# Attention and gated MLP in float32: start addresses of matmul operands modulo 512 bytes, and an order of the first wave with sums and exponentials one step behind what feeds them

## The chip, the cores and the metric

One core of a Trainium2 chip runs the whole program. The metric is the device time of one execution in microseconds; the median of three runs is compared. The engines that matter here are TensorE (PE; its weight loads are PEld), VectorE (DVE), ScalarE (ACT), GpSimd (POOL, which here issues DMAs), and SyncE (SP, whose queue issues the other DMAs).

## The reference

Attention without a score matrix, and a gated MLP on its output, for 8 batches of 576 tokens (4608 tokens in all), 8 heads of 64, model width 512 and inner width 1536:

```python
q_s = exp(q - max(q, axis=-1));  q_s = q_s / (sum(q_s, axis=-1) + 1e-9)
k_s = exp(k - max(k, axis=2));   k_s = k_s / (sum(k_s, axis=2) + 1e-9)
kv  = einsum('bhsd,bhse->bhde', k_s, v)
x   = einsum('bhsd,bhde->bhse', q_s, kv)      # tokens x 512
gate = 1 / (1 + exp(-(x @ w_gate)))           # 512 -> 1536
out  = (gate * (x @ w_val)) @ w_out           # 1536 -> 512
```

## The kernel before

The 4608 tokens are nine **waves** of 512. A wave has its x (four blocks of 128 channels by 512 tokens, tile x_32), then the two up projections, the gate, and the down projection into four PSUM accumulators.

**Waves 1 to 8** keep precision by splitting each float32 operand into a high part and a remainder, both of type float32r, and by multiplying high by high, high by low and low by high (function prod, line 635, and line 703). A wave runs six steps, p = 0 to 5. Function g1 computes one step's two projections with seven products of half size instead of eight: the weights are three blocks as they are (tile a_w, kept in SBUF for all six steps) and four sums or differences of blocks (tile s_sb, one step at a time, read back from HBM by s_load right after its last use); the moving operands are c_hl, the x of the wave in seven parts. A product is 12 matmuls with 128 x 128 weights and 256 moving columns, a step 84 (line 635). Function g2 multiplies the result h of one step by the down weights: 24 matmuls (line 703), weights h, 512 moving columns of wo_hl, of which two tiles per step are read back from HBM: the first twelve matmuls stream one of tag wo_hl, the last twelve one of tag wo_t. Between the steps stand the matmuls that make the next wave's x: k_mm (line 358, weights k, moving v) and x_mm (line 518, weights kv_sb, moving the split q in tiles of the pool ring). Where a wave crosses a batch, x_mm works in two pieces of columns, and the second begins inside the tile: in wave 1 at column 64, byte 256.

**Wave 0** prepares all this. It runs plain float32 matmuls, 12 steps j: g1_0(j) (line 590), then g2_0(j - 1) (line 617), whose weights are h_0, the product of gate and value that VectorE makes in g_mul_0(j - 1) (line 602). Beside them each step narrows the next weights from 64-bit input words to float32 (w_low, w_top, w_join and their wo_ counterparts; narrow_sign on ScalarE, line 143), makes for each pair of steps the four sums (w_sums, line 235), splits sums and blocks into high and low (split_w, copies on ScalarE on line 222, subtractions on VectorE on line 223), saves s_sb to HBM (line 250), splits and saves wo (lines 201, 205), and computes the attention of wave 1 (after_first: the subtractions of q on line 433, the exponentials of q on 437, those of k on 293 and 337).

Nothing reorders instructions: each engine executes in the order in which the program is written (manual_schedule), and an instruction that waits holds all that stand behind it on its engine. Where a tile lies in SBUF follows from the order of the pools and of the tiles in them; the tiles named pad are never used, they only move what comes behind them.

## Time and profile before

| | |
|---|---|
| median of 3 runs | 1000.17 us (997.86 to 1000.83) |
| the profiled execution | 999.88 us, span 998.0 us |
| TensorE busy, its weight loads | 964.4 us, 832.2 us |
| VectorE, ScalarE, GpSimd busy | 610.5, 475.7, 167.4 us |
| matmuls of line 635, of line 703 | 4032 of 256 columns, 1152 of 512 |
| mean DMA rate | 258 GB/s |

The span runs from the first to the last instruction; the execution's own time is 1.9 us more. Times in rows are us from the start of the span unless ns is written. A duration of a matmul includes its way through the array, so that matmuls overlap in the record; how fast they follow each other is read from the starts.

### The profile page before, as it was taken

Reading aid. Unit: us, or ns where it says so; the run is one execution under the profiler, and the core shown is the slowest. Engines: PE = TensorE matmul, PEld = TensorE weight load, DVE = VectorE, ACT = ScalarE, POOL = GpSimd, SP = SyncE. Lnnn points to the kernel's source line nnn. Section 1 sums busy time; section 2 is a strip of 40 time slices with the busy share of each in tenths; the row PEclk is TensorE's granted clock in tenths of the full one; section 3 lists DMA queues with packets and bytes.
Section 4 is the critical chain, followed back from the end, with each engine's and each line's share of the span. In section 5 each row is a group of like instructions: output and inputs, shape, how many; then the busy total and the mean of one; then the engine's idle time right before and its main releaser. Section 6 shows DMA issues by size and latency. Waiting matters only on the chain.

```text
span 998.0 us, 15641 instructions
## 1 busy us (share of the span) xinstructions
PE 964.4 (97%) x6062; PEld 832.2 (83%) x6062; DVE 610.5 (61%) x1010; ACT 475.7 (48%) x815; POOL 167.4 (17%) x316
## 2 busy tenths in 40 slices
PE   5895999999999999999999999999999999999998
PEld 4432544699999999899999999999999999999997
DVE  8696778676566556745675567547663655463242
ACT  4679596453436254525453544353444434533222
POOL 0010001221122112112111111121212121212210
PEclk7998999999999999999999999999999999999999
DMA  9867567898699978997899789987998679858662
GB/s 347 311 173 309 227 240 214 294 353 271 198 236 360 306 223 194 375 294 242 166 384 321 236 151 379 321 255 139 385 304 231 212 227 314 241 178 252 191 207 73
DMA packets 93865, 257.79 MB, mean 258 GB/s; under 512 B 15264, under 2 KB 17568, under 8 KB 93024
## 3 DMA queue, kind: packets, MB, share of 16 engines
q0 software_dynamic: 43712, 168.32, 56.1%
q1 hardware_dynamic: 50080, 88.48, 29.7%
q8 instruction: 48, 0.79, 0.4%
q14 instruction: 25, 0.20, 0.1%
HBM read 228.20 MB, written 28.56 MB: 257 GB/s over the span
## 4 chain that ended last, share of the span: by engine, by line
PE 84%; ACT 8%; DMA 5%; DVE 2%; issue 1%; SPq 0%; ACTq 0%; DVEq 0%
PE gv L635 46%; PE acc L703 23%; PE gv L590 5%; PE acc L617 3%; PE at L358 3%; PE gv L518 2%; ACT ring L337 2%; DMA sg<-wv_in 1%; ACT ring L437 1%; DMA lent<-kT_in 1%; PE at L518 1%; ACT kt L293 1%; DMA ring<-k_in 1%; ACT L437 1%; DMA lent<-v_in 1%
## 5 line engine op out<-in xcount | busy, mean ns | idle before, releaser
L635 PE MATMUL gv<-c_hl,s_sb 128*128 128x256 f32 x2304 | 293.6, 283 | 1.8 <-ACT sg L653 1.8
L635 PEld LDWEIGHTS gv<-c_hl,s_sb 128*128 128x128 f32 x2304 | 283.6, 192 | 3.1 <-ACT sg L653 3.1
L703 PE MATMUL acc<-wo_hl,h 128*128 128x512 f32 x1152 | 274.5, 393 | 0.0
L703 PEld LDWEIGHTS acc<-wo_hl,h 128*128 128x128 f32 x1152 | 212.9, 188 | 47.2
L635 PE MATMUL gv<-c_hl,a_w 128*128 128x256 f32 x1728 | 231.4, 283 | 0.0
L635 PEld LDWEIGHTS gv<-c_hl,a_w 128*128 128x128 f32 x1728 | 220.2, 192 | 4.1 <-issue 0.7
L258 POOL DMA_DIRECT2D s_sb<-s x188 | 99.7, 530 | 330.1 <-PE gv L635 327.1
L661 DVE TENSOR_TENSOR sg<-gv,sg 128x512 f32<-128x512 f32 x48 | 33.2, 691 | 188.1 <-PE gv L635 188.1
L217 POOL DMA_DIRECT2D wo_hl<-wo x96 | 50.9, 530 | 304.4 <-PE acc L703 301.7
L663 ACT COPY sg<-gv 128x512 f32<-128x512 f32 x48 | 28.2, 587 | 110.1 <-PE gv L635 110.1
L590 PE MATMUL gv<-x,f_w 128*128 128x512 f32 x160 | 72.4, 605 | 4.7 <-ACT h L598 4.7
L653 ACT COPY sg<-gv 128x512 f32<-128x512 f32 x48 | 28.1, 585 | 101.9 <-PE gv L635 78.4
L665 DVE TENSOR_TENSOR sg<-sg 128x512 f32<-128x512 f32 x48 | 33.3, 693 | 61.9 <-ACT sg L663 61.9
L590 PEld LDWEIGHTS gv<-x,f_w 128*128 128x128 f32 x160 | 30.5, 194 | 43.1 <-issue 36.0
L686 DVE TENSOR_TENSOR h<-sg,h 128x1024 fp32r<-128x1024 f32 x48 | 58.8, 1226 | 1.6
L668 ACT ACTIVATE sg<-sg 128x512 f32<-128x512 f32 x48 | 30.4, 632 | 57.6 <-DVE sg L667 57.6
L617 PE MATMUL acc<-wo_t,h 128*128 128x512 f32 x96 | 46.4, 629 | 11.2 <-DVE h L602 11.2
L674 DVE TENSOR_TENSOR sg<-sg 128x512 f32<-128x512 f32 x48 | 33.2, 692 | 33.5 <-ACT sg L668 33.5
L617 PEld LDWEIGHTS acc<-wo_t,h 128*128 128x128 f32 x96 | 19.0, 202 | 36.3 <-issue 21.8
L658 ACT COPY sg<-gv 128x512 f32<-128x512 f32 x48 | 28.2, 587 | 43.6 <-PE gv L635 43.6
L655 ACT COPY sg<-gv 128x512 f32<-128x512 f32 x48 | 28.1, 586 | 32.3 <-PE gv L635 32.3
L667 DVE TENSOR_TENSOR sg<-gv,sg 128x512 f32<-128x512 f32 x48 | 33.2, 692 | 6.2
(151 smaller groups left out, 1021.1 us busy)
## 6 DMA issues: line engine op xcount, KB each, us to landing
s_sb<-s POOLq DMA_DIRECT2D x188, 512.0 KB, 6.7
wo_hl<-wo POOLq DMA_DIRECT2D x96, 512.0 KB, 5.7
s<-s_sb POOLq DMA_DIRECT2D x6, 2048.0 KB, 8.1
out<-x SPq DMA_DIRECT2D x36, 256.0 KB, 8.8
ring<-k_in SPq DMA_DIRECT2D x28, 256.0 KB, 14.3
ring<-qn_in SPq DMA_DIRECT2D x28, 256.0 KB, 9.8
q_b<-q_m_row SPq DMA_DIRECT2D x56, 128.0 KB, 7.9
ring<-qT_in SPq DMA_DIRECT2D x28, 256.0 KB, 9.2
```

The lines of the kernel that those rows point to most:

```text
L217: nc.gpsimd.dma_start(out=t.rearrange("p h e -> p (h e)"), in_=wo_dram[2 * p + i].bitcast(F32R))
L258: nc.gpsimd.dma_start(out=s_sb[:, i].rearrange("p h n e -> p (h n e)"), in_=s_dram[p][:, i * n:(i + 1) * n].bitcast(F32R),)
L590: nc.tensor.matmul(ps[n], lhsT=w[:, kt // 2, sl], rhs=x_0[:, kt], start=(kt == 0), stop=(kt == NK - 1),)
L617: nc.tensor.matmul(acc[0][m], lhsT=h_0[j][:, m * P:(m + 1) * P], rhs=wo_t[j // 2][:, j % 2], start=(j == 0), stop=(j == NJ - 1),)
L635: nc.tensor.matmul(ps[:, n], lhsT=lh(kt), rhs=c_hl[i][:, x, kt], start=(first and n == 0 and kt == 0 and lh is wh and x == 0), stop=(last ...
L661: nc.vector.tensor_tensor(out=sg[:, 0], in0=rr, in1=sg[:, 0], op=ALU.add)
L665: nc.vector.tensor_tensor(out=sg[:, 3], in0=sg[:, 3], in1=sg[:, 2], op=ALU.add)
L667: nc.vector.tensor_tensor(out=sg[:, 1], in0=z, in1=sg[:, 1], op=ALU.add)
L668: nc.scalar.activation(sg[:, 0:2, 0], sg[:, 0:2, 0], AF.Sigmoid)
L674: tt(out=sg[:, 0:2, 0], in0=sg[:, 0:2, 0], in1=sg[:, 0:2, 1], op=ALU.mult)
L686: nc.vector.tensor_tensor(out=lo, in0=sg[:, :, 0], in1=hi.bitcast(F32), op=ALU.subtract)
L703: nc.tensor.matmul(acc[w][m], lhsT=h[lh][:, i, sl], rhs=o[i][:, rh], start=(at == 0 and i == 0 and lh == 0 and rh == 0), stop=(at == NS - ...
```

## The change

It has two parts.

**Addresses.** The pools are put in another order, and two pads of 192 and 320 bytes a partition stand elsewhere, so that tiles begin at other addresses. Small tiles for the maxima of k get a pool of their own. No instruction changes by it. First byte of each tile within a partition, modulo 512, as the built programs have it:

| operand | used as | before | after |
|---|---|---|---|
| a_w, s_sb (line 635) | weights | 0 | 128 |
| c_hl (line 635) | moving | 0 | 448 |
| h (line 703) | weights | 0 | 128 |
| wo_hl, first of a step (line 703) | moving | 192 | 448 |
| wo_hl, second of a step, tag wo_t (line 703) | moving | 0 | 448 |
| kv_sb (line 518) | weights | 0 | 128 |
| q in ring (line 518) | moving | 0 | 448 |
| f_w, h_0 (wave 0) | weights | 0 | 128 |
| x_0, wo_t (wave 0) | moving | 0 | 448 |
| k in ring (line 358) | weights | 0 | 448 |
| v (line 358) | moving | 0 | 128 |

All slices that these matmuls take are multiples of 512 bytes into their tile, but for the second pieces of line 518.

**Order of wave 0.** split_w becomes split_hi (copies) and split_lo (subtractions). They run at steps 2, 4, 6, 8, 10 and 11 instead of 1, 3, 5, 7, 9 and 11, and split_hi stands ahead of the step's other work on ScalarE. The sums run at steps 1, 3, 5, 7, 9 and 10 instead of 0, 2, 4, 6, 8 and 10. The exponentials of q and the key sums of wave 1 move from step 2 to 3, the subtractions of k stay in 3, the sums over q move from 3 to 4. For odd j the sign bits of wo come from one more operation on VectorE (narrow_sign_bits) instead of one on ScalarE.

On ScalarE at steps 2 and 3, from the gate of step 2 (h_484 before, h_488 after; h_542 and h_538 are the gates of step 3) the order before is

```order
L598 ACTIVATE h_484<-gv 128x512
L437 ACT_TABLE_LOAD
L437 ACTIVATE ring<-ring 128x512 x4
L293 ACTIVATE lent,k_sum<-lent,k_neg 128x576 x4
L201 CAST wo_hl<-wo_t 128x512
L143 ACTIVATE w_raw<-w_raw 128x1024
L151 ACTIVATE f_w<-w_raw 128x2x256 x2
L143 ACTIVATE wo_raw<-wo_raw 128x512
L151 ACTIVATE wo_t<-wo_raw 128x512
L598 ACT_TABLE_LOAD
L598 ACTIVATE h_542<-gv 128x512
L222 CAST s_sb<-s_492 128x512
```

and after

```order
L615 ACTIVATE h_488<-gv 128x512
L215 CAST wo_hl<-wo_t 128x512
L147 ACTIVATE w_raw<-w_raw 128x1024
L162 ACTIVATE f_w<-w_raw 128x2x256 x2
L147 ACTIVATE wo_raw<-wo_raw 128x512
L162 ACTIVATE wo_t<-wo_raw 128x512
L615 ACTIVATE h_538<-gv 128x512
L454 ACT_TABLE_LOAD
L454 ACTIVATE ring<-ring 128x512 x4
L310 ACTIVATE lent,k_sum<-lent,k_neg 128x576 x4
L262 CAST s_sb<-s_547 128x512
L262 CAST s_sb<-s_548 128x512
```

The table load, the four exponentials of q (ring) and the four of k (lent) have moved behind the gate of step 3, and the copies of the split stand behind them.

On VectorE at step 10, from the product of step 10 (h_949 before, h_953 after) the order before is

```order
L602 TENSOR_TENSOR h_949<-gv,h_949 128x512
L205 TENSOR_TENSOR wo_hl<-wo_t,wo_hl 128x512
L235 TENSOR_TENSOR s_1001<-f_last 128x512
L235 TENSOR_TENSOR s_1002<-s_1001,f_last 128x512
L235 TENSOR_TENSOR s_1003<-f_last 128x512
L235 TENSOR_TENSOR s_1004<-f_last,s_1002 128x512
L560 TENSOR_TENSOR ring<-x_89 128x512
L560 TENSOR_TENSOR ring<-x_89,ring 128x512
L560 TENSOR_TENSOR ring<-x_89 128x512
L560 TENSOR_TENSOR ring<-x_89,ring 128x512
```

and after

```order
L619 TENSOR_TENSOR h_953<-gv,h_953 128x512
L219 TENSOR_TENSOR wo_hl<-wo_t,wo_hl 128x512
L266 TENSOR_TENSOR s_sb<-s_957,s_sb 128x512
L266 TENSOR_TENSOR s_sb<-s_958,s_sb 128x512
L266 TENSOR_TENSOR s_sb<-s_959,s_sb 128x512
L266 TENSOR_TENSOR s_sb<-s_960,s_sb 128x512
L266 TENSOR_TENSOR a_w<-f_w,a_w 128x2x512
L266 TENSOR_TENSOR a_w<-f_w,a_w 128x512
L243 TENSOR_TENSOR s_1012<-f_last 128x512
L243 TENSOR_TENSOR s_1013<-s_1012,f_last 128x512
L243 TENSOR_TENSOR s_1014<-f_last 128x512
L243 TENSOR_TENSOR s_1015<-f_last,s_1013 128x512
```

The subtractions of split 4 (s_sb, a_w) now stand between the save of wo_hl and the sums of the last pair; before, they stood ahead of the product.

The diff, without empty lines:

```diff
@@ -53,20 +53,25 @@
     nc = tc.nc
     const = ctx.enter_context(tc.tile_pool(name="const", bufs=1))
+    cpool = ctx.enter_context(tc.tile_pool(name="cpool", bufs=1))
+    apad = ctx.enter_context(tc.tile_pool(name="apad", bufs=1))
     apool = ctx.enter_context(tc.tile_pool(name="apool", bufs=1))
     two = ctx.enter_context(tc.tile_pool(name="two", bufs=2))
-    pad = ctx.enter_context(tc.tile_pool(name="pad", bufs=1))
-    pad.tile([P, 80], F32, name="pad_2")
+    wpad = ctx.enter_context(tc.tile_pool(name="wpad", bufs=1))
+    wpool = ctx.enter_context(tc.tile_pool(name="wpool", bufs=2))
     four = ctx.enter_context(tc.tile_pool(name="four", bufs=4))
     ring = ctx.enter_context(tc.tile_pool(name="ring", bufs=11))
+    small = ctx.enter_context(tc.tile_pool(name="small", bufs=2))
+    apad.tile([P, 48], F32, name="pad_a")
+    wpad.tile([P, 80], F32, name="pad_w")
     dpool = ctx.enter_context(tc.tile_pool(name="dpool", bufs=2, space=bass.MemoryType.DRAM))
     spool = ctx.enter_context(tc.tile_pool(name="spool", bufs=1, space=bass.MemoryType.DRAM))
     ps_acc = ctx.enter_context(tc.tile_pool(name="ps_acc", bufs=NT, space=bass.MemoryType.PSUM))
     ps_gv = ctx.enter_context(tc.tile_pool(name="ps_gv", bufs=3, space=bass.MemoryType.PSUM))
     ps_at = ctx.enter_context(tc.tile_pool(name="ps_at", bufs=1, space=bass.MemoryType.PSUM))
-    const.tile([P, 96], F32, name="pad_0")
     s_sb = const.tile([P, 4, 2, 2, 2 * P], F32R, name="s_sb")
     x_32 = const.tile([P, NP, T], F32, name="x_32")
     sg = const.tile([P, 4, 2, HT], F32, name="sg")
@@ -85,7 +90,6 @@
     )
     ident = const.tile([P, P], F32, name="ident")
     make_identity(nc, ident)
-    const.tile([P, 48], F32, name="pad_1")
     ctx.enter_context(tc.manual_schedule())
@@ -113,7 +117,7 @@
             return sg.rearrange("p q n t -> p (q n t)").bitcast(I32)
         if i == 3:
             return x_32.rearrange("p h t -> p (h t)").bitcast(I32)
-        return apool.tile([P, 4 * DM], I32, name="w_raw", tag=f"c{i}")
+        return cpool.tile([P, 4 * DM], I32, name="w_raw", tag=f"c{i}")
     def load_w(j):
         w_raw[j] = t = raw_tile(j).rearrange("p (n e) -> p n e", n=2)
@@ -122,7 +126,7 @@
     def load_wo(j):
         if j % 3 == 0:
-            wo_raw[j] = t = apool.tile([P, 2 * DM], I32, name="wo_raw", tag="c3")
+            wo_raw[j] = t = cpool.tile([P, 2 * DM], I32, name="wo_raw", tag="c3")
         else:
             wo_raw[j] = t = two.tile([P, 2 * DM], I32, name="wo_raw", tag="h_hi")
         nc.sync.dma_start(out=t, in_=wo[j * P:(j + 1) * P].bitcast(I32))
@@ -142,6 +146,13 @@
         half = raw.bitcast(F16).rearrange("p (e f) -> p e f", f=4)
         nc.scalar.activation(
             half[:, :, 1], words(raw)[:, :, 1].bitcast(F32), AF.Copy, scale=2.0 ** -100
+        )
+    def narrow_sign_bits(raw):
+        hi, low = (words(raw)[:, :, i] for i in (1, 0))
+        nc.vector.scalar_tensor_tensor(
+            out=low, in0=hi, scalar=-2 ** 31, in1=low,
+            op0=ALU.bitwise_and, op1=ALU.bitwise_or,
         )
     def narrow_abs(raw, w):
@@ -184,11 +195,14 @@
     def wo_low(j):
         narrow_low(wo_raw[j])
+        if j % 2:
+            narrow_sign_bits(wo_raw[j])
     def wo_top(j):
         if j % 2 == 0:
-            wo_t[j // 2] = two.tile([P, 2, DM], F32, name="wo_t")
-        narrow_sign(wo_raw[j])
+            wo_t[j // 2] = wpool.tile([P, 2, DM], F32, name="wo_t")
+        if j % 2 == 0:
+            narrow_sign(wo_raw[j])
         narrow_abs(wo_raw[j], wo_t[j // 2][:, j % 2])
     def wo_join(j):
@@ -197,7 +211,7 @@
     wo_out = {}
     def wo_hi(j):
-        wo_out[j] = t = two.tile([P, 2, DM], F32R, name="wo_hl")
+        wo_out[j] = t = wpool.tile([P, 2, DM], F32R, name="wo_hl")
         nc.scalar.copy(out=t[:, 0], in_=wo_t[j // 2][:, j % 2])
     def wo_save(j):
@@ -211,19 +225,13 @@
     def wo_load(w, p):
         wo_hl[w, p] = [
-            two.tile([P, 2, DM], F32R, name="wo_hl", tag=tag) for tag in ("wo_hl", "wo_t")
+            wpool.tile([P, 2, DM], F32R, name="wo_hl", tag=tag) for tag in ("wo_hl", "wo_t")
         ]
         for i, t in enumerate(wo_hl[w, p]):
             nc.gpsimd.dma_start(
                 out=t.rearrange("p h e -> p (h e)"), in_=wo_dram[2 * p + i].bitcast(F32R)
             )
-    def parts(o, x):
-        nc.scalar.copy(out=o[:, :, 0], in_=x)
-        nc.vector.tensor_tensor(
-            out=o[:, :, 1], in0=x, in1=o[:, :, 0].bitcast(F32), op=ALU.subtract
-        )
     s_32 = {}
     def w_sums(p):
@@ -239,19 +247,28 @@
         tt(S3, f[:, 0], f[:, 2], ALU.subtract)
         tt(S4, f[:, 1], t[S2][:, 0], ALU.subtract)
-    def split_w(p):
+    def split_of(p):
         f = f_w[p].rearrange("p b n e -> p b (n e)")
         s = s_sb.rearrange("p s h n e -> p s h (n e)")
+        a = a_w[p].rearrange("p b h n e -> p b h (n e)")
+        return [(s[:, i:i + 1], t) for i, t in enumerate(s_32[p])] + [
+            (a[:, A11:A12 + 1], f[:, 0:2]), (a[:, A22:A22 + 1], f[:, 3:4])
+        ]
+    def split_hi(p):
         a_w[p] = apool.tile([P, 3, 2, 2, 2 * P], F32R, name="a_w", tag=f"a{p}")
-        a = a_w[p].rearrange("p b h n e -> p b h (n e)")
-        for i, t in enumerate(s_32.pop(p)):
-            parts(s[:, i:i + 1], t)
+        for o, x in split_of(p):
+            nc.scalar.copy(out=o[:, :, 0], in_=x)
+    def split_lo(p):
+        for o, x in split_of(p):
+            nc.vector.tensor_tensor(
+                out=o[:, :, 1], in0=x, in1=o[:, :, 0].bitcast(F32), op=ALU.subtract
+            )
         nc.gpsimd.dma_start(
             out=s_dram[p], in_=s_sb.rearrange("p s h n e -> p (s h n e)").bitcast(F32)
         )
-        parts(a[:, A11:A12 + 1], f[:, 0:2])
-        parts(a[:, A22:A22 + 1], f[:, 3:4])
     def s_load(p, i):
         n = 4 * 2 * P
@@ -280,7 +297,7 @@
     def k_max(b, hp):
         if hp == 0:
             kmax[b], kneg[b], ksum[b] = (
-                two.tile([P, NP], F32, name=f"k_{x}") for x in ("max", "neg", "sum")
+                small.tile([P, NP], F32, name=f"k_{x}") for x in ("max", "neg", "sum")
             )
         m = kmax[b][:, hp:hp + 1]
         nc.vector.tensor_reduce(out=m, in_=kT_sb[b, hp], axis=AX.X, op=ALU.max)
@@ -525,7 +542,7 @@
         copy(out=x_32[:, hp], in_=x_ps.pop((w, hp)))
-    x_0 = apool.tile([P, NP, T], F32, name="x_0", tag="c2")
+    x_0 = cpool.tile([P, NP, T], F32, name="x_0", tag="c2")
     q_0 = [two.tile([P, 2, T], F32, name="q_0", tag="h_lo") for _ in range(2)]
     def qT_copy(hp):
@@ -566,7 +583,7 @@
     def c_split(i):
         if i % 2 == 0:
-            t = apool.tile([P, 2 if i < 6 else 1, 2, 2, HT], F32R, name="c_hl", tag=f"c{i // 2}")
+            t = cpool.tile([P, 2 if i < 6 else 1, 2, 2, HT], F32R, name="c_hl", tag=f"c{i // 2}")
             for x in range(i, min(i + 2, 7)):
                 c_hl[x] = t[:, x % 2]
         src = c_32.pop(i) if i in c_32 else quarter(*{B11: (0, 0), B21: (1, 0), B22: (1, 1)}[i])
@@ -816,18 +833,18 @@
         if j == 2:
             for c in range(NC):
                 qn_sub(1, c)
+        if j == 3:
             for c in range(NC):
                 qn_exp(1, c)
             for hp in range(NP):
                 k_sum(1, hp)
-        if j == 3:
             for t in range(5):
                 k_sub(1, t)
-            for c in range(NC):
-                qn_sum(1, c)
         if j == 4:
             for t in range(5):
                 k_exp(1, t)
+            for c in range(NC):
+                qn_sum(1, c)
             for hp in range(NP):
                 qf_mul(1, hp)
         if j == 5:
@@ -985,13 +1002,16 @@
     for j in range(NJ):
         g1_0(j)
         beside_first(j)
+        p = j // 2 if j == NJ - 1 else j // 2 - 1
+        split = j > 0 and (j % 2 == 0 or j == NJ - 1)
+        if split:
+            split_hi(p)
         if j > 0:
             wo_hi(j - 1)
         if j + 2 < NJ:
             w_top(j + 2)
         if j + 1 < NJ:
             w_join(j + 1)
-        if j + 1 < NJ:
             wo_top(j + 1)
         wo_join(j)
         if j > 0:
@@ -1009,9 +1029,9 @@
             load_w(j + 5)
         if j == 7:
             load_w(NJ - 1)
-        if j % 2:
-            split_w(j // 2)
-        else:
+        if split:
+            split_lo(p)
+        if j % 2 and j < NJ - 1 or j == NJ - 2:
             w_sums(j // 2)
         if j > 0:
             g2_0(j - 1)
```

## Rows read from the trace of the kernel before

**Rows 1.** Chain of work that ended last, whole span: its shares by line
```profile
PE gv L635 46%; PE acc L703 23%; PE gv L590 5%; PE acc L617 3%; PE at L358 3%; PE gv L518 2%; ACT ring L337 2%; DMA sg<-wv_in 1%; ACT ring L437 1%; DMA lent<-kT_in 1%; PE at L518 1%; ACT kt L293 1%; DMA ring<-k_in 1%; ACT L437 1%; DMA lent<-v_in 1%
```

**Rows 2.** Instruction groups, whole span: count | busy us, mean ns | idle
```profile
L635 PE MATMUL gv<-c_hl,s_sb 128*128 128x256 f32 x2304 | 293.6, 283 | 1.8 <-ACT sg L653 1.8
L703 PE MATMUL acc<-wo_hl,h 128*128 128x512 f32 x1152 | 274.5, 393 | 0.0
L635 PE MATMUL gv<-c_hl,a_w 128*128 128x256 f32 x1728 | 231.4, 283 | 0.0
```

**Rows 3.** Waits of TensorE from 186 us on: total us, times, longest
```profile
PE gv L635 <- ACT sg L653: 1.8, 6, 0.5
```

**Rows 4.** Timeline of TensorE, 501 to 512 us: start us, us, group
```profile
501.00 5.71 PE L703 MATMUL acc<-wo_hl,h 128*128 128x512 f32 x24
506.55 1.60 PE L635 MATMUL gv<-c_hl,a_w 128*128 128x256 f32 x12
507.98 3.04 PE L635 MATMUL gv<-c_hl,s_sb 128*128 128x256 f32 x24
510.86 1.36 PE L635 MATMUL gv<-c_hl,a_w 128*128 128x256 f32 x10
```

**Rows 5.** L703 by shape, 502.2 to 503.5 us, first twelve (wo_hl at 192)
```profile
L703 PE MATMUL acc<-wo_hl,h 128*128 128x512 f32 x7 | 1.8, 394 | 0.0
```

**Rows 6.** The same, 505.25 to 506.25 us, last twelve (wo_hl at 0)
```profile
L703 PE MATMUL acc<-wo_hl,h 128*128 128x512 f32 x6 | 1.5, 389 | 0.0
```

**Rows 7.** L518 of wave 1 by shape, two stretches (moving operand at 256)
```profile
L518 PE MATMUL at<-ring,kv_sb 128*128 128x448 f32 x3 | 0.9, 393 | 0.0
...
L518 PE MATMUL at<-ring,kv_sb 128*128 128x448 f32 x3 | 0.8, 389 | 0.0
```

**Rows 8.** The same of wave 7, 782.1 to 782.6 us (at 0)
```profile
L518 PE MATMUL at<-ring,kv_sb 128*128 128x448 f32 x3 | 0.9, 394 | 0.0
```

**Rows 9.** Timeline of TensorE, 114 to 117 us, matmuls of 128 columns
```profile
114.03 1.95 PE L358 MATMUL at<-v,ring 128*128 128x128 f32 x16
115.81 1.06 PE L358 MATMUL at<-lent,ring 128*128 128x128 f32 x8
```

**Rows 10.** TensorE in wave 0; in brackets idle time before, who ended it
```profile
47.77 5.40 PE L590 MATMUL gv<-x,f_w 128*128 128x512 f32 x8 [3.45 <-ACT h L598]
...
54.89 3.70 PE L617 MATMUL acc<-wo_t,h 128*128 128x512 f32 x8 [1.72 <-DVE h L602]
...
97.21 6.68 PE L617 MATMUL acc<-wo_t,h 128*128 128x512 f32 x8 [9.50 <-DVE h L602]
...
110.59 3.60 PE L617 MATMUL acc<-wo_t,h 128*128 128x512 f32 x8
```

**Rows 11.** Timeline of ScalarE, step 2 of wave 0
```profile
71.03 2.43 ACT L437 ACTIVATE ring<-ring 128x512 f32<-128x512 f32 x4 [5.46 <-DVE ring L433]
```

**Rows 12.** Stretch; busy PE, PEld, DVE, ACT, POOL; clock, DMA, GB/s; then VectorE
```profile
54.15:107.05 52.90, 41.46 (x88) 17.66 (x89) 44.12 (x76) 44.95 (x61) 4.29 (x7) 0.90 0.74 254
...
84.50 2.50 DVE L223 TENSOR_TENSOR s_sb<-s,s_sb 128x512 fp32r<-128x512 f32 x4 [6.77 <-ACT s_sb L222]
```

**Rows 13.** Timeline, end of wave 0: ScalarE, then TensorE
```profile
161.13 2.23 ACT L222 CAST s_sb<-s 128x512 fp32r<-128x512 f32 x4
...
164.23 1.50 PE L518 MATMUL at<-ring,kv_sb 128*128 128x64 f32 x6
165.56 7.03 PE L590 MATMUL gv<-x,f_last 128*128 128x512 f32 x16
172.43 3.60 PE L617 MATMUL acc<-wo_t,h 128*128 128x512 f32 x8
...
182.73 3.60 PE L617 MATMUL acc<-wo_t,h 128*128 128x512 f32 x8
```

**Rows 14.** DMA issues: count, KB each, us to landing
```profile
s<-s_sb POOLq DMA_DIRECT2D x6, 2048.0 KB, 8.1
```

**Rows 15.** Busy time by engine in wave 5, columns as in rows 12
```profile
592.00:693.50 101.50, 101.23 (x709) 94.73 (x708) 62.61 (x106) 45.41 (x85) 18.60 (x36) 1.00 0.98 273
```

## The prediction

> **What bounds the kernel now.** I read the chain of work that ended last, then the groups of instructions, then the waits of TensorE by stage. The chain is TensorE: lines L635 and L703, the matmuls of waves 1 to 8, hold 69% of the span [rows 1]. From 186 us to the end TensorE waits 1.8 us for others in all [rows 3]. So what one matmul costs there sets the time, and wave 0 (the first 186 us), where TensorE does wait, is a second and smaller account.
>
> The unit cost is read from starts, not from durations (a record of 283 or 393 ns spans more than the engine's time for one, [rows 2]). In [rows 4] 24 matmuls of 256 columns start at 507.98 and the next group starts at 510.86: 120.0 ns each. The 24 of 512 columns between 501.00 and 506.55 take 231 ns each, but they are two kinds. All have weights (h) that begin at 0 modulo 512 bytes; the first twelve stream a wo_hl that begins at 192, the last twelve one that begins at 0. Their records last 394 ns [rows 5] and 389 ns [rows 6]. With the group's 5.55 us that is about 233 and 227 ns apart (12 x 233 + 12 x 227 = 5.52 us). Same shape, same engine, same stretch: **the start address costs something**, some 6 ns in 230. At 2.4 GHz 512 columns are 213 ns and 256 are 107 ns, so 13 to 20 ns of each matmul are not streaming. Matmuls of 128 columns, whose pace is set by the weight load, run 16 in 115.81 - 114.03 = 1.78 us, 111 ns each [rows 9]: a 256-wide one can't be expected below that.
>
> **Part 1, the addresses.** Nothing is added; tiles move. In waves 1 to 8 the moving operand begins 0 (or, for half of L703, 192) bytes after the weights modulo 512 before, and 320 bytes after it everywhere now. No row shows 320. Three rows bound it:
> - 0: 120 ns at 256 columns, 227 at 512 [rows 4, 6].
> - 192: 233 at 512 [rows 5], so +6.
> - 256: L518 of wave 1 streams 448 columns that begin at 256; groups of three average 393 and 389 ns [rows 7], 391 in the mean. In wave 7 the same shape begins at 0 and averages 394 [rows 8]. The first of three is set by the 64-wide ones ahead of it, so the difference of 3 sits on two: -4.5 each.
>
> The moving operand is read at twice the rate of the weights (256 columns beside a load of 128), so it gains 512 bytes on the weights during one load. A start 192 ahead meets them after 320/512 of the load, 256 ahead after half, 320 ahead after 192/512. From 192 to 256 the cost falls by 10 ns; 320 is the next step the same way. I take the row at 256, -4.5 ns, for all. It is as near to 320 as the row at 192 is, and this choice is the weak point. The sum: 4032 matmuls of L635 x 4.5 = 18.1 us; 576 of L703 from 227, 2.6 us; 576 from 233, 10.5 ns each, 6.0 us; 180 of L518, 0.8 us. Together **-27.5 us**. The bounds: if 256 columns fall to the 111 ns of [rows 9], 4032 x 9 = 36 us, and if 512 lose as much from 227 and 233, 5 and 9 us more: -50. If all become as the row at 192 (+6 on L635 and on half of L703), 24.2 + 3.5 + 1.1 = +29.
>
> The Trainium skill, "TensorE: Matmul & The Clock Gate", section "Wait — 56ns, not 53.3ns?", puts warm matmuls N/2.4 GHz + 2.5 ns apart, 109 and 216 ns here. By that figure the most to be won would be an estimated 44 us on L635 and 16 us on L703; the traced 120 and 227 to 233 lie above it.
>
> What hides behind the faster matmuls stays hidden: in a wave of 101.5 us VectorE is busy 62.6 and ScalarE 45.4 [rows 15], and a wave would shrink by some 3.4 us. DMA, at a share of 0.98 [rows 15], is the one to watch: were 1.00 a ceiling, a wave could not go under 99.5 us, and eight waves would give 16 us and not 27.5: 980. Against that, TensorE waits for no transfer now [rows 3]; I keep 980 inside the range. The wave-0 matmuls (float32, two passes each) take 6.87 us for sixteen passes of 512 columns, 429 ns each [rows 13]: at one column per two cycles of 2.4 GHz that is 427 and no excess, so I count nothing there.
>
> **Part 2, wave 0.** Each step j of wave 0 needs h of step j-1 from VectorE. Now, at step 2, the exponentials wait on ScalarE for subtractions that VectorE does last in that step: 5.46 us idle [rows 11]. Everything behind them on ScalarE is late, the copies of split_w(1) among it, and the subtractions that need these hold VectorE 6.77 us [rows 12]. The product for step 4 stands behind them, and TensorE waits 9.50 us at 97.21 [rows 10]. The change puts exponentials and key sums a step behind the subtractions, and copies and subtractions of the split a step behind the sums, so both waits go.
>
> What is late next is VectorE's own queue. From the start of step 1's product to the start of step 5's, 54.15 to 107.05, are 52.90 us, of which VectorE was busy 44.12 [rows 12]. The new order holds the same work there (one set of sums comes in, one goes out) plus two sign operations of about 0.6 us (a pass of VectorE over 512 elements, four in 2.50, [rows 12]), and without the idle time it is done in 45.3: the product of step 5 starts at 99.5 and ends at 100.2. TensorE, no longer held at 97.21, wants it at about 96.1 (54.89 [rows 10] and four steps of 10.30, the distance from 172.43 to 182.73 in [rows 13]) and waits some 4 us. It starts on it at 100.2 where it started at 110.59 [rows 10]: 10.4 us won. After a wait of 3.45 us eight passes took 5.40 us [rows 10] where others take 3.60 [rows 13]: 1.8 us of lower clock (the granted clock over this stretch was 0.90, [rows 12]), which I subtract for the new wait: 8.6.
>
> At the end of wave 0 some is **given back**. The last two splits are now one step apart (10 and 11), where all were two apart. From the end of L518 at 165.73 (164.23 + 1.50, [rows 13]), in times of before: ScalarE's eviction 0.5, the copies of split 4 now ahead of wo_hi, 2.2 + 1.6 (four in 2.23, [rows 13], and three more units of that size), wo_hi 0.5: 170.4. VectorE then does wo_save 0.6, split 4.2 (seven units of 0.6), sums 2.4, differences 2.4, four halves 2.4, join and product 1.2: 183.6, against 182.73 [rows 13] where TensorE wants it: 0.9 us. The copies of split 5 overwrite s_sb, so they wait until its save has landed: subtracted at 173.4, plus 8.1 us [rows 14], 181.5, plus 0.5 to issue. Then copies 3.7 and subtractions 4.2: a_w is whole at 190, wanted at 187.1: 2.9 us. So 3.8 us go back. Net 8.6 - 3.8 = -4.8; with the small idle times that a real queue has I take **-4 us**, between -10 (no wait at the end) and +2 (a landing as late as 14 us). The six sign operations moved from ScalarE to VectorE are in these sums. Of the queues, SP's loads keep their places; the save that the split issues moves a step down GpSimd's, past the step's save of wo_hl alone. Later than 186 us nothing of part 2 runs.
>
> **Sum.** The profiled execution took 999.88 us (span 998.0), 0.3 under the median of 1000.17. 999.9 - 27.5 - 4 = **968 us**.
>
> **Rivals.** (a) *The address decides nothing more*: 320 costs what 0 costs. For it: L635 is 120.0 over whole groups, steady as an engine's own rate. Against it: [rows 5] and [rows 6]. L703's first half falls to 227, 576 x 6 = 3.5 us, and wave 0 gives 4: 992. The Trainium skill, "SBUF — State Buffer", section "Who interferes with whom", gives TensorE two independent read ports, one for moving operands and one for weights, and has it wait on nobody. By that rule no start address changes anything, the two halves of L703 should be equal, which they are not here, and only wave 0 would move: 996 us.
> (b) *Distance counts, not direction* (slower): 320 ahead is 192 behind, and costs what 192 costs [rows 5]. Then 120 becomes 126 and 227 becomes 233: 999.9 + 29 - 4 = 1025. It decides as soon as L635 is above 121 ns, since 4032 x 1 ns outweighs wave 0. For it: the one clean pair of rows with unequal starts is the slow one. Against it: the rows at 256.
> (c) *The change of order does not do what it says*: the wait at 97.21 only moves to the next product and the end of wave 0 takes back all. It changes the forecast by 4 us, to 972, and is inside the range.
>
> **How the numbers follow.** Forecast (faster matmuls, 946 to 985) 0.48; (a) 0.22, at 990 to 998; (b) 0.30, at 1005 to 1030. The range takes the lower bound less its last tenth, 947, to (b) with its wave 0 unhelped, 1028. A measurement of this kernel tells about 0.3% from no change, 3 us: (a) lies below 997 in about seven of ten cases. Faster 0.48 + 0.15 = 0.63, same 0.08, slower 0.29.
>
> **What would show it.** Right: twelve 256-wide matmuls of L635's group in 1.39 us or less (1.44 now), both halves of L703 alike and at or under 385 ns, no wait near 9 us in wave 0, a wait of some 4 us at the next product, and the first L635 some 4 us earlier. Wrong: L635's spacing still 120.0 (a), or 126 and both halves of L703 at 394 (b). TensorE waits for s_sb or wo_hl after 186 us would mean that the DMA queues have taken over.

## The result and the profile after

The changed kernel takes 989.06 us (median of 4 runs, 987.87 to 991.24) against 1000.5 us (median of 4): a ratio of 0.9894, 95% interval 0.9868 to 0.9919. It is faster, by 11 us where 32 were forecast. The profiled execution took 988.35 us, its span 986.5.

The rows of the page that answer to [rows 2] (line 635 is now L652, line 703 L720; count | busy us, mean ns | idle):

```profile
L652 PE MATMUL gv<-c_hl,s_sb 128*128 128x256 f32 x2304 | 288.3, 280 | 4.0 <-ACT sg L670 3.9
L720 PE MATMUL acc<-wo_hl,h 128*128 128x512 f32 x1152 | 272.1, 392 | 0.0
L652 PE MATMUL gv<-c_hl,a_w 128*128 128x256 f32 x1728 | 226.2, 279 | 2.5 <-DVE a_w L266 2.5
```

Records are 3 to 4 ns shorter in L652 and 1 ns in L720. The paces are in the timeline of TensorE (start us, us, group), which answers to [rows 4]; first a stretch of wave 4, then one of wave 5:

```profile
504.74 2.88 PE L652 MATMUL gv<-c_hl,s_sb 128*128 128x256 f32 x24
507.46 1.52 PE L652 MATMUL gv<-c_hl,a_w 128*128 128x256 f32 x12
...
518.39 1.52 PE L652 MATMUL gv<-c_hl,a_w 128*128 128x256 f32 x12
519.75 1.52 PE L652 MATMUL gv<-c_hl,s_sb 128*128 128x256 f32 x12
521.82 1.68 PE L652 MATMUL gv<-c_hl,s_sb 128*128 128x256 f32 x12 [0.55 <-ACT sg L670]
523.35 1.57 PE L652 MATMUL gv<-c_hl,a_w 128*128 128x256 f32 x12
```

```profile
604.72 1.58 PE L652 MATMUL gv<-c_hl,a_w 128*128 128x256 f32 x12
606.14 2.99 PE L652 MATMUL gv<-c_hl,s_sb 128*128 128x256 f32 x24
608.96 1.58 PE L652 MATMUL gv<-c_hl,a_w 128*128 128x256 f32 x12
...
614.62 5.66 PE L720 MATMUL acc<-wo_hl,h 128*128 128x512 f32 x24
620.11 1.58 PE L652 MATMUL gv<-c_hl,a_w 128*128 128x256 f32 x12
```

The same line, the same addresses, **two paces**: 24 matmuls from 504.74 to 507.46 are 113.3 ns each, 24 from 606.14 to 608.96 are 117.5 (117.8 over longer stretches). Stretches of products run at the one or the other. The pace changes where TensorE has waited, as at 521.82, but also behind output products without a wait: the step that starts at 286.35 ends at 117.7, the next, at 301.88, runs at 113.3. Of the 336 products of waves 1 to 8, 100 run at 113.3 and 198 at 117.8; the other 38, those with waits among them, average neither. L720 takes 229 ns in both its halves (614.62 to 620.11 is 24 of them).

Wave 0, TensorE, then three stretches (stretch; busy PE, PEld, DVE, ACT, POOL; granted clock, DMA share, GB/s), then ScalarE (ahead of 97 us, and at the end of wave 0) and VectorE; they answer to [rows 10, 12, 13]:

```profile
97.14 5.40 PE L607 MATMUL gv<-x,f_w 128*128 128x512 f32 x8 [2.48 <-ACT h L615]
105.74 3.70 PE L634 MATMUL acc<-wo_t,h 128*128 128x512 f32 x8 [3.20 <-DVE h L619]
...
179.27 3.70 PE L634 MATMUL acc<-wo_t,h 128*128 128x512 f32 x8 [1.11 <-DVE h L619]
182.41 0.80 PE L652 MATMUL gv<-c_hl,a_w 128*128 128x256 f32 x2
185.74 1.97 PE L652 MATMUL gv<-c_hl,a_w 128*128 128x256 f32 x10 [2.53 <-DVE a_w L266]
187.50 4.03 PE L652 MATMUL gv<-c_hl,s_sb 128*128 128x256 f32 x24
```

```profile
54.30:105.00 50.70, 43.96 (x96) 18.48 (x96) 45.48 (x78) 39.91 (x58) 3.76 (x7) 0.97 0.75 266
...
186.50:189.70 3.20, 3.20 (x17) 3.20 (x17) 2.79 (x5) 0.58 (x1) 0.00 (x0) 0.50 0.99 410
189.90:197.00 7.10, 7.10 (x62) 7.10 (x62) 2.08 (x3) 2.22 (x4) 2.87 (x6) 1.00 0.98 287
```

```profile
74.38 0.62 ACT L215 CAST wo_hl<-wo_t 128x512 fp32r<-128x512 f32 x1 [7.48 <-DVE ring L450]
...
87.05 2.16 ACT L262 CAST s_sb<-s 128x512 fp32r<-128x512 f32 x4
90.59 0.61 ACT L215 CAST wo_hl<-wo_t 128x512 fp32r<-128x512 f32 x1
...
177.25 2.18 ACT L262 CAST s_sb<-s 128x512 fp32r<-128x512 f32 x4 [1.67 <-DMA s<-s_sb]
```

```profile
66.79 0.43 DVE L140 TENSOR_SCALAR wo_raw<-wo_raw 128x512 uint32<-128x512 uint32 x1 [1.60 <-DMA wo_raw<-wo_in]
...
91.23 0.69 DVE L219 TENSOR_TENSOR wo_hl<-wo_t,wo_hl 128x512 fp32r<-128x512 f32 x1 [3.30 <-ACT wo_hl L215]
```

The first L652 starts at 182.41, 3.35 us earlier than before, but two matmuls later TensorE waits 2.53 us for a_w. Behind that wait the granted clock is 0.50, the lower of its two levels (1.2 and 2.4 GHz), from 186.5 to 189.7 us, and 1.00 again from 189.9 on. The second step of wave 1 starts at 200.06, where it started at 199.27: wave 0 gave nothing. From there to the end the kernel before took 798.7 us and the kernel after 786.5, so the whole gain lies behind wave 0, where the addresses alone differ.

### The profile page after: what moved, and what is told of

Its sections match the earlier page's. It is cut to its first block, busy times and chain, and to the rows that moved or that the text cites. A ratio compares the mean times of both kernels' runs of the same rounds, so it can differ in the third digit from the quotient of the medians.

```text
span 986.5 us, 15628 instructions
## 1 busy us (share of the span) xinstructions
PE 951.7 (96%) x6062; PEld 821.9 (83%) x6062; DVE 615.2 (62%) x1016; ACT 468.3 (47%) x809; POOL 166.8 (17%) x316
## 4 chain that ended last, share of the span: by engine, by line
PE 72%; DMA 14%; ACT 8%; DVE 4%; issue 1%; SPq 1%; DVEq 0%; ACTq 0%
PE gv L652 41%; PE acc L720 21%; DMA ring<-k_in 4%; PE gv L607 3%; DMA q_m_row<-q_m 2%; PE at L375 2%; PE acc L634 2%; DMA ring<-qT_in 2%; PE gv L535 2%; DMA q_b<-q_m_row 2%; DMA wo_raw<-wo_in 1%; ACT ring L454 1%; DMA lent<-kT_in 1%; ACT ring L354 1%; PE at L535 1%
## 5 line engine op out<-in xcount | busy, mean ns | idle before, releaser
L652 PE MATMUL gv<-c_hl,s_sb 128*128 128x256 f32 x2304 | 288.3, 280 | 4.0 <-ACT sg L670 3.9
L652 PEld LDWEIGHTS gv<-c_hl,s_sb 128*128 128x128 f32 x2304 | 277.2, 188 | 6.5 <-ACT sg L670 6.2
L720 PE MATMUL acc<-wo_hl,h 128*128 128x512 f32 x1152 | 272.1, 392 | 0.0
L720 PEld LDWEIGHTS acc<-wo_hl,h 128*128 128x128 f32 x1152 | 212.9, 188 | 44.4
L652 PE MATMUL gv<-c_hl,a_w 128*128 128x256 f32 x1728 | 226.2, 279 | 2.5 <-DVE a_w L266 2.5
L652 PEld LDWEIGHTS gv<-c_hl,a_w 128*128 128x128 f32 x1728 | 214.9, 188 | 7.0 <-DVE a_w L266 2.7
L678 DVE TENSOR_TENSOR sg<-gv,sg 128x512 f32<-128x512 f32 x48 | 33.2, 692 | 171.9 <-PE gv L652 171.9
L703 DVE TENSOR_TENSOR h<-sg,h 128x1024 fp32r<-128x1024 f32 x48 | 58.8, 1226 | 1.6
L634 PE MATMUL acc<-wo_t,h 128*128 128x512 f32 x96 | 43.6, 596 | 8.6 <-DVE h L619 8.6
L672 ACT COPY sg<-gv 128x512 f32<-128x512 f32 x48 | 28.1, 585 | 27.7 <-PE gv L652 27.5
L409 ACT CAST kv_sb<-kmax_b 64x256 fp32r<-64x256 f32 x14 | 5.7, 404 | 67.9 <-DVE kmax_b L385 67.6
```

The source lines that it names most:

```text
L634: nc.tensor.matmul(acc[0][m], lhsT=h_0[j][:, m * P:(m + 1) * P], rhs=wo_t[j // 2][:, j % 2], start=(j == 0), stop=(j == NJ - 1),)
L652: nc.tensor.matmul(ps[:, n], lhsT=lh(kt), rhs=c_hl[i][:, x, kt], start=(first and n == 0 and kt == 0 and lh is wh and x == 0), stop=(last ...
L678: nc.vector.tensor_tensor(out=sg[:, 0], in0=rr, in1=sg[:, 0], op=ALU.add)
L703: nc.vector.tensor_tensor(out=lo, in0=sg[:, :, 0], in1=hi.bitcast(F32), op=ALU.subtract)
L720: nc.tensor.matmul(acc[w][m], lhsT=h[lh][:, i, sl], rhs=o[i][:, rh], start=(at == 0 and i == 0 and lh == 0 and rh == 0), stop=(at == NS - ...
```

## The experiments

**The two parts apart.** e1_addresses is before with the new pools alone, e2_order is after with the old ones:

```diff
-    pad.tile([P, 80], F32, name="pad_2")
+    cpool = ctx.enter_context(tc.tile_pool(name="cpool", bufs=1))
...
+    wpool = ctx.enter_context(tc.tile_pool(name="wpool", bufs=2))
...
+    apad.tile([P, 48], F32, name="pad_a")
+    wpad.tile([P, 80], F32, name="pad_w")
```

> The kernel before with the new pools and pads alone: every weight tile begins at 128 and every moving tile at 448 modulo 512, the order of wave 0 as before. Theory A (the addresses made the whole gain, and the new order of wave 0 nets nothing): 988 us, between 986 and 991; the products of the sums at 117.8 or 113.3 ns per matmul of 256 columns, the output products near 229 ns in both halves; in wave 0 the 9.5 us wait at 97 us stands. Theory B (the gain came with the new order): 1000 us, 120.0 ns. Theory C (both count, the order some 4 us as I had forecast): 993 us.

Measured: 988.12 us, ratio 0.9884 (0.9864 to 0.9904), -11.6 us by the ratio. From the second step of wave 1 to the end it took 785.5 us. In its profiled execution, 984.17 us (the five lie between 983.75 and 989.27), 151 products run at 113.3 and 148 at 117.8, at the addresses of the kernel after with its 100 and 198: the addresses allow the two paces, but do not fix the share of each.

> The kernel after with the pools and pads of before: the new order of wave 0 alone, distances 0 and 192 as before. Theory A: 1000 us, between 998.5 and 1002, 120.0 ns per matmul of 256 columns, 227 and 233 ns in the two halves of the output products; the first product of wave 1 some 3 us earlier and its second step no earlier. Theory B: 988 us. Theory C: 996 us.

Measured: 1001.54 us, ratio 1.0024 (1.0014 to 1.0034), +2.4 us by the ratio; 120.0 ns in L652's place, 233 and 227 ns in the halves of L720's, 798.5 us from the second step of wave 1 on. Theory A: the addresses made the gain, and the new order costs a little.

**The distance by itself.** m1_table leaves the kernel's work out and runs blocks of 36 matmuls, weights at w, moving operand at m modulo 512:

```diff
+    pairs = [(W[0], m) for m in M] + [(W[1], m) for m in M[::2]]
...
+    for w, m in pairs:
+        block(w, m, 256, ps_two)
...
+    for w, m in pairs:
+        block(w, m, 512, ps_two)
```

> The disputed cost by itself: blocks of 36 matmuls on an otherwise idle core, 24 pairs of a weight tile (at 0 or 128) and a moving tile (at 0, 32, ... 480), first 256 columns without waits, then 256 columns with a wait ahead of each block, in the one order and in the reverse, then 512 columns. The rest of the kernel's work is left out. Theory A1 (the distance modulo 512 alone): weights 0 with moving 320 run as weights 128 with moving 448, at 113 to 118 ns; distance 0 at 120.0 (256 columns) and 227 (512); distance 192 at 126 and 233. Theory A2 (the places themselves): the same distance gives two paces. Theory A3 (the pace comes from the other traffic of the kernel): all blocks alike. If the two paces of 113.3 and 117.8 are chosen at a restart, the blocks behind a wait differ between the two orders; if they are chosen by what ran just ahead, the blocks without waits do too.

Measured, ns from start to start (mean of the last 32 gaps of a block), by (m - w) modulo 512; the second of a pair of rows has the distance 256 greater:

```
distance              0    32    64    96   128   160   192   224
256 cols, no wait  120.0 117.8 117.8 119.8 118.7 117.4 113.8 118.3
  the same, +256   119.8 117.8 117.8 119.8 118.7 117.4 113.8 118.3
512 cols           227.0 233.3 228.8 233.8 233.3 234.4 233.3 233.3
  the same, +256   227.0 233.3 228.8 233.7 233.3 234.4 233.3 233.3
weights at 128, 256 cols: distance 320 117.8, 192 113.4, 0 119.7
```

Theory A1 holds with a correction: the pace goes by the difference of the two starts **modulo 256**, not 512, and not by the places (weights at 0 and at 128 agree within 0.5 ns at 256 columns and 1.2 at 512); so 256 costs what 0 costs. The two widths rank the distances differently: 192 is among the slow ones at 512 columns and the fastest at 256. With a wait ahead of a block, those at 192 and 448 ran at 113.3 to 113.5 in two of eight and at 117.8 in six; each other distance kept its pace within 1.2 ns. The Trainium skill, "SBUF — State Buffer", section "Who interferes with whom", has the two read ports of TensorE independent; here blocks that differ in an address alone on an otherwise idle core take 113.4 to 120.0 ns, and the measurement decides.

**The row that I took the price from.** d256 is after with all that moves at 384, a distance of 256:

```diff
+    cpad.tile([P, 112], F32, name="pad_c")
-    apad.tile([P, 48], F32, name="pad_a")
-    wpad.tile([P, 80], F32, name="pad_w")
+    apad.tile([P, 64], F32, name="pad_a")
+    wpad.tile([P, 64], F32, name="pad_w")
```

> The kernel after, with all moving tiles at 384 and the weights still at 128: a distance of 256, that of the row from which I took 4.5 ns. If that row (3 us in 780, of three 448-wide matmuls) read the start address rightly, 115.5 ns per matmul of 256 columns and near 975 us. If it read something else (the 64-wide ones beside it), a pace between 113 and 120 that has nothing to do with 4.5, and a time from 975 to 1000.

Measured: 998.07 us, in a single execution. Its timeline of TensorE:

```profile
496.50 3.04 PE L654 MATMUL gv<-c_hl,s_sb 128*128 128x256 f32 x24
499.38 1.60 PE L654 MATMUL gv<-c_hl,a_w 128*128 128x256 f32 x12
500.82 5.63 PE L722 MATMUL acc<-wo_hl,h 128*128 128x512 f32 x24
506.28 1.60 PE L654 MATMUL gv<-c_hl,a_w 128*128 128x256 f32 x12
```

From 496.50 to 499.38 are 24 matmuls of 120.0 ns, from 500.82 to 506.28 24 of 227.5. At 256 nothing is won in L654; only the half of L722 that stood at 192 before is. The 3 ns between [rows 7] and [rows 8] are not the address either. [rows 7] shows two of the four groups of wave 1; the other two, first here, average 395 and 391, so that all four average 392 against the 394 of [rows 8]. In d256 the distances are exchanged, and the records stay: the last group of wave 1 (now at 0) has its 389, that of wave 7 (now at 256) its 394:

```profile
L518 PE MATMUL at<-ring,kv_sb 128*128 128x448 f32 x3 | 0.9, 395 | 0.0
...
L518 PE MATMUL at<-ring,kv_sb 128*128 128x448 f32 x3 | 0.9, 391 | 0.0
```

```profile
L537 PE MATMUL at<-ring,kv_sb 128*128 128x448 f32 x3 | 0.8, 389 | 0.0
...
L537 PE MATMUL at<-ring,kv_sb 128*128 128x448 f32 x3 | 0.9, 394 | 0.0
```

**The wave-0 order taken apart**, on the old addresses. e3_exp moves only the exponentials, the key sums and the sums over q, e4_sign adds the sign operations, e5_first_splits and e6_last_splits add the splits of either end (copies, subtractions and, for the first four, the sums). Differences between these runs are of medians:

```diff
         if j == 2:
             for c in range(NC):
                 qn_sub(1, c)
+        if j == 3:
             for c in range(NC):
                 qn_exp(1, c)
```

Against e2_order, e5_first_splits (splits 4 and 5 in steps 9 and 11, as before), then e6_last_splits (splits 0 to 3 in steps 1, 3, 5 and 7, as before):

```diff
-        p = j // 2 if j == NJ - 1 else j // 2 - 1
+        p = {2: 0, 4: 1, 6: 2, 8: 3}.get(j)
...
-        p = j // 2 if j == NJ - 1 else j // 2 - 1
+        p = {10: 4, 11: 5}.get(j)
```

> The kernel before with that one move of the exponentials alone, addresses as before. Theory W1: 992 to 996 us. Theory W2: 1000 us within 2. Theory W3 (ScalarE's idle 5.46 us only moves to the next step): the wait at 97 us stays above 7 us, and the time is that of before.

Measured: 993.9 us, 0.9949 (0.9934 to 0.9965). W1: the exponentials are worth 5.5 us, and TensorE's 9.50 us at the product for step 4 become 2.14 there and 1.42 at the next.

> The run labelled e3_exp with the sign operations of six of the twelve blocks of w_out moved from ScalarE to VectorE, as in the kernel after; the splits stay as before. With it the new order of wave 0 is taken apart: e3_exp is the exponentials alone, this one adds the signs, the run labelled e2_order adds the splits. Theory H (the splits a step behind, with the last two one step apart, give the gain back): 994 us within 1.5, so that the splits alone cost 7 us. Rival I (VectorE is the late engine in wave 0, six operations of 0.6 us more on it delay the products): 997 to 1001.

Measured: 992.08 us, 0.9930 (0.9918 to 0.9943). Neither: the signs do not cost; the 1.8 us by which the run lies under e3_exp are not clear of noise (the intervals overlap).

> The new order of wave 0 on the old addresses, but only the first four splits stand a step behind their sums; the last two stand in steps 9 and 11 as before. Theory H (the last two, one step apart, cost the time: the first product of wave 1 waits for a_w and runs on at a lower clock): 992 to 994 us, no wait for a_w at the end of wave 0. Rival J (the copies of any split ahead of the step's other work on ScalarE cost the time): 997 us or more.

Measured: 995.99 us, 0.9967 (0.9954 to 0.9980).

> The complement: the first four splits as before, the last two in steps 10 and 11 as in the kernel after, one step apart. Theory H: 998 to 1002 us, with a wait of 2 to 3 us for a_w and a first step of wave 1 of some 18 us where it takes 13.5 otherwise. Rival J: 994 to 996.

Measured: 997.1 us, 0.9986 (0.9975 to 0.9996). So from e4_sign the first four splits cost 3.9 us, the last two 5.0, both 9.5 (e2_order): H and J are each half right, and the costs add up to within 0.6 us. The end of wave 0 in e6_last_splits, TensorE and clock:

```profile
178.50 0.80 PE L647 MATMUL gv<-c_hl,a_w 128*128 128x256 f32 x2
182.17 2.33 PE L647 MATMUL gv<-c_hl,a_w 128*128 128x256 f32 x10 [2.87 <-DVE a_w L261]
184.30 3.69 PE L647 MATMUL gv<-c_hl,s_sb 128*128 128x256 f32 x24
...
196.62 2.00 PE L647 MATMUL gv<-c_hl,a_w 128*128 128x256 f32 x12
```

```profile
182.40:185.70 3.30, 3.30 (x17) 3.30 (x17) 3.30 (x6) 0.59 (x1) 0.00 (x0) 0.50 1.07 447
```

The step takes 18.12 us where it took 13.51: 2.87 us of waiting, and 1.7 us more for matmuls at the lower level of the clock, granted 0.50, behind the wait. In e5_first_splits TensorE waits for nothing from 165 to 200 us, and the step takes 13.51.

**Using the table.** mix puts c_hl at 64 (distance 192 modulo 256) and wo_hl at 128 (distance 0), in the order of before; mix_exp adds the exponentials of e3_exp; mix64 has wo_hl at 192 (distance 64). mix against e1_addresses, and mix64 against mix_exp:

```diff
+    cpad.tile([P, 32], F32, name="pad_c")
-    apad.tile([P, 48], F32, name="pad_a")
-    wpad.tile([P, 80], F32, name="pad_w")
+    apad.tile([P, 16], F32, name="pad_a")
...
+    wpad.tile([P, 16], F32, name="pad_w")
```

> The order of before, weights at 128 everywhere; what the products of waves 1 to 8 stream (256 columns) at 64, a distance of 192 modulo 256, and what the output products stream (512 columns) at 128, a distance of 0. Theory D (the table of blocks holds inside the kernel: the pace goes by the distance modulo 256 and by the width): 256 columns at 113.3 or 117.8 ns, 512 columns at 227 in both halves; all at 117.8 gives 988 us, all at 113.3 gives 970, so between 970 and 985. Rival E (192 ahead is costly at every width, as rows 5 read at 512 columns): 126 ns and over 1015 us.

Measured: 986.81 us, 0.9873 (0.9854 to 0.9892), just above D's range: the paces are the table's, 227 ns in both halves of the output products, but 200 products ran at 117.8 and 95 at 113.3 (in the profiled execution, at 989.16 us the longest of five).

> The same, and of the new order only that the exponentials and key sums of wave 0 stand a step behind the subtractions; the splits stay with the sums, two steps apart. Theory W1 (the exponentials alone held the queue; what gave the gain back was the last two splits one step apart): 4 to 8 us under the run labelled mix, the wait of 9.5 us at 97 us under 4 us, no wait for a split weight at the end of wave 0. Theory W2 (any earlier start is given back at the end of wave 0): within 2 us of mix.

Measured: 981.87 us, 0.9826 (0.9812 to 0.9839). W1, 4.9 us under mix. Its timeline shows where the pace changes:

```profile
509.38 1.58 PE L638 MATMUL gv<-c_hl,a_w 128*128 128x256 f32 x12
510.80 1.58 PE L638 MATMUL gv<-c_hl,s_sb 128*128 128x256 f32 x12
512.82 1.65 PE L638 MATMUL gv<-c_hl,s_sb 128*128 128x256 f32 x12 [0.44 <-ACT sg L656]
514.30 1.52 PE L638 MATMUL gv<-c_hl,a_w 128*128 128x256 f32 x12
```

Behind the output products a step starts at 117.8 (12 in 1.42 us); behind the wait it is 113.3 (514.30 to 515.66), as behind most waits. Steps that follow output products and have no wait stay at 117.8.

> What sets 113.3 or 117.8 by itself, the kernel's other work left out: steps of 12 matmuls of 256 columns, a wait of varied length (16 lengths), 36 matmuls of 256 columns, 12 of 512 columns at distance 0; at distance 64 and at 192; then the same with one extra matmul of 64, 128 or 512 columns behind the wait. Theory F (the phase between weight load and streaming at the restart selects the pace, and it holds until the next restart): at each distance some blocks at 113.3 and some at 117.8, by the length of the wait, and one kind of extra matmul turns most to one pace. Theory G (the distance decides: 64 is 117.8 and 192 is 113.3, and waits only disturb for some matmuls): 64 always 117.8, 192 always 113.3 within 12 matmuls of the wait.

```diff
+        run(a, m, 256, 12)
...
+        run(b, m, 256, 36)
+        o = ps_two.tile([P, DM], F32, name="o")
+        run(o, 0, 512, 12)
```

Measured: the lengths did not vary (0.94 us from start to start across every wait), so the part on the length of a wait stays untried. Behind the 512-wide group both distances run at 117.8. Behind the bare wait, distance 192 ran at 113.3 in 16 of 16, distance 64 at 117.8 in 16 of 16; an extra matmul of 128 columns turned 64 to 113.3 in 8 of 16; one of 64 left 192 at 117.8 in 16 of 16. Between F and G: what runs just ahead picks one of two paces, and which ahead picks which depends on the distance.

> As mix_exp, but what the output products stream begins at 192: distance 64 (228.9 ns in the table of blocks) in place of 0 (227). Theory F (the pace of a 256-wide group is the one at which the stream ahead of it ran; a 512-wide group at distance 0 sets 117.8, one at distance 64 keeps what it found, as in the last five steps of the run labelled e1_addresses; a wait at distance 192 sets 113.3): after the first wait nearly all products of waves 2 to 8 run at 113.3, 1152 x 2 ns = 2 us go to the output products, some 200 products x 12 x 4.5 ns = 11 us come back: 972 us, between 970 and 976. Rival: the 512-wide group sets 117.8 at whatever distance: 984, two above mix_exp.

Measured: 983.6 us, 0.9856 (0.9831 to 0.9880). The rival: a 512-wide group at distance 64 also leaves the 256-wide ones at distance 192 at 117.8, 197 products against 190 in mix_exp.

> Groups of 12 matmuls of 512 columns and then 36 of 256, without waits, the kernel's other work left out; the 256-wide ones at distance 64 and 192, the 512-wide ones at 0 and (last) at 64; the last matmul of 512 or the first of 256 is cut in two in ten ways. Theory F: a plain 512-wide group at distance 0 leaves the 256-wide ones at 117.8; some cut leaves them at 113.3, and a 512-wide group at 64 keeps the pace it found. Rival: no cut changes anything, and only a wait does.

```diff
+        for n in end:
+            one(o, om, lo, n, False, lo + n == 512)
+            lo += n
...
+        for n in begin:
+            one(a, m, lo, n, lo == 0, False)
+            lo += n
```

Measured, at distance 192, behind a 512-wide group at 0: the plain group leaves 117.8; the last 512 cut into 256 and 256, 384 and 128, 128 and 384, or 448 and 64, or the first 256 cut into 128 and 128 or 192 and 64, leaves 113.3, each in 4 of 4; the other four cuts leave 117.8. At distance 64 behind a group at 0 no cut helps. At distance 64 behind a group at 64, the distances of the kernel after, plain groups kept the pace that they found: they ran at 117.8 in 4 of 4; with the first 256 cut into halves the pace turned to 113.3 at the second of four groups; plain groups behind these stayed at 113.3 in 4 of 4, and the last 512 cut into halves changed the pace each time. Timeline at distance 192, two groups behind a plain 512, two behind the cut into halves (36 matmuls, 4.40 and 4.26 us):

```profile
469.71 4.40 PE L82 MATMUL a<-m,w 128*128 128x256 f32 x36
473.95 2.88 PE L82 MATMUL o<-m,w 128*128 128x512 f32 x12
476.67 4.40 PE L82 MATMUL a<-m,w 128*128 128x256 f32 x36
480.91 2.89 PE L82 MATMUL o<-m,w 128*128 128x512 f32 x13
483.64 4.26 PE L82 MATMUL a<-m,w 128*128 128x256 f32 x36
487.74 2.90 PE L82 MATMUL o<-m,w 128*128 128x512 f32 x13
490.48 4.26 PE L82 MATMUL a<-m,w 128*128 128x256 f32 x36
```

**A version that beats both.** mix_cut cuts the last of each step's 24 matmuls of 512 columns, which makes 25; best adds the signs:

```diff
+                    cut = 2 if i == 1 and m == NT - 1 and lh == 1 else 1
+                    for c in range(cut):
+                        cols = slice(c * DM // cut, (c + 1) * DM // cut)
                         nc.tensor.matmul(
-                            acc[w][m], lhsT=h[lh][:, i, sl], rhs=o[i][:, rh],
+                            acc[w][m][:, cols], lhsT=h[lh][:, i, sl], rhs=o[i][:, rh, cols],
```

> mix_exp with the last of each step's 24 matmuls of 512 columns cut into two of 256 (47 more matmuls, of some 6 ns each). Theory F (the two matmuls ahead of a group choose its pace; in the blocks that cut left the 256-wide group at distance 192 at 113.3 in all cases, the whole 512 at 117.8): the products that ran at 117.8 in mix_exp (190 of 336) run at 113.3, 190 x 12 x 4.5 ns = 10 us, less 48 x 0.02 us: 973 us, between 970 and 976. Rival (in the kernel the waits decide, not the entry): 982, as mix_exp.

Measured: 975.4 us, 0.9777 (0.9758 to 0.9797), 5 us under mix_exp by the ratios and 6.5 by the medians; 36 products at 117.8 are left. Its timeline:

```profile
502.93 5.62 PE L709 MATMUL acc<-wo_hl,h 128*128 128x512 f32 x25
508.39 1.54 PE L638 MATMUL gv<-c_hl,a_w 128*128 128x256 f32 x12
509.77 1.52 PE L638 MATMUL gv<-c_hl,s_sb 128*128 128x256 f32 x12
511.86 1.68 PE L638 MATMUL gv<-c_hl,s_sb 128*128 128x256 f32 x12 [0.56 <-ACT sg L656]
513.38 1.58 PE L638 MATMUL gv<-c_hl,a_w 128*128 128x256 f32 x12
```

Behind the cut group a step starts at 115 ns (508.39 to 509.77) and is at 113.3 from then on, up to the next wait. A wait leaves 113.3 in most steps, but not here (513.38 is followed by a start at 514.79: 117.5). Theory F holds for the entry; for waits it predicts too much.

> mix_cut with the sign operations of e4_sign: if both add up, 975.4 - 1.8 = 973.6 us; if the shorter wave 0 is given back at its end, 975.4.

Measured: 976.26 us, 0.9769 (0.9757 to 0.9782): the same as mix_cut within the noise; a gain from the signs is not seen here, and 1.8 us would be too small to be told.

## Why the prediction was wrong

The forecast was 968, from -27.5 for the addresses and -4 for wave 0; measured are -11.6 (e1_addresses) and +2.4 (e2_order). The time lies inside the range, and that it lies near rival (a)'s 992 is luck: 320 does not cost what 0 costs. The signs named ahead came out mixed: a product's twelve matmuls took 1.36 us in 100 products and 1.41 in 198, where 1.39 or less was asked for; both halves of the output products are alike, but their records average 392 ns and not 385; the wait near 9 us went, and the next product waited 3.20.

- **What bounds the kernel**: right. All that was won was won in TensorE's pace from 199 us on, and TensorE waits little there: 3.9 us for ScalarE after, 1.8 before [rows 3].
- **The start address costs something** [rows 5, 6]: right, and shown by m1_table.
- **The price of 320** failed, and this is the step that decides. "From 192 to 256 the cost falls by 10 ns; 320 is the next step the same way" assumed a smooth course over 512 bytes. The cost has a period of 256, 320 is 64, and 256 is 0. The row at 256 that I took for all was no effect of the address at all: of four groups I had taken two, and d256 shows the same records with the distances exchanged. Sized by the term, with the starts of TensorE's matmuls summed from the second step of wave 1 to the end: L635's 18.1 us became 9.8 (477.3 us before, 467.5 after; 100 x 12 x 6.7 + 198 x 12 x 2.2 ns would be 13.3, and waits for ScalarE, 2.1 us more than before, and the matmuls just behind waits take the rest); L703's 8.6 became 2.3 (266.6 and 264.3), since 229 stands between the 227 and 233 of before; L518's 0.8 is lost in the 0.2 by which all other matmuls changed. Together 12.3 us in place of 27.5.
- **One price for both widths** failed too: carrying the 6 ns of 512 columns to 256 (in rival (b)) has the wrong sign, since 192 is the fastest distance at 256 columns.
- **One pace for one address** was taken for granted, not said. 113.3 and 117.8 are both paces of the same line at the same addresses, and the difference, 4.5 ns on half of L652, is 9 us.
- **Wave 0, the won part**: the 9.50 us at 97.21 went, and the next product waited 3.20 us (some 4 forecast), but it started at 105.74, not at 100.2. The step that failed is "without the idle time it is done in 45.3". The work was as forecast: from step 1's product to step 5's, 54.30 to 105.00, VectorE is busy 45.48 us. But 5.2 us of idle time stayed, which the sum had left out: 1.60 for a load of wo_raw at 66.79, and 3.30 for ScalarE at 91.23. ScalarE still idles 7.48 us in step 2, now ahead of a copy of wo_t (what ends this is open: the profile names the subtractions of q here, the save of wo_hl in e2_order), then does the exponentials and the new copies of the split (87.05 to 90.59) ahead of wo_hi, for which VectorE stands. e5_first_splits prices the move of the first four splits as a whole, copies, subtractions and sums: 3.9 us. That the copies alone make it is argued from these rows, not run by itself. The 1.8 us of lower clock came one group earlier, behind the wait of 2.48 us at 97.14 (5.40 us for eight passes); the 0.90 that stands beside this term is the mean of 54.15 to 107.05, and the passes from which it was taken began ahead of that, at 47.77.
- **Wave 0, the part given back**: 0.9 us at step 10's product was 1.11, and 2.9 us for a_w was 2.53, behind a save landing as I had it (1.67 us of ScalarE's wait at 177.25). What the sum lacks is the lower clock behind the wait (0.50 from 186.5 to 189.7), which I had charged for the other wait: the step that holds it takes 17.65 us after, against 13.51 before. e6_last_splits prices the whole: 5.0 us.
- **Rival (c)**, that wave 0 takes back all, is what part 2 did; it was priced right, to within the 2.4 us by which it overshot.

Not settled: why the paces have these values, what tips a step at distance 64 to 113.3 in the kernel, what decides which pace a wait leaves, and how the share of the two paces comes to differ between executions.

## What to carry to other kernels

Before a price is taken from two rows that differ in one thing, ask what else differs in them, and whether the course between them is known: here a block of 36 matmuls for each distance cost one run and replaced the whole argument. A wait of TensorE can cost more than its length, as the two at a_w did: look at the granted clock behind it and charge the slower matmuls as well. An order that removes one engine's wait must be walked through on the other engine's queue too, instruction by instruction, before the gain is counted.
